# Sliding-window attention and a two-layer MLP on one core: a new order of three entries in the opening's list of transfers, and new planner constants

## The chip, the cores and the metric

The kernel runs on one core of a Trainium2 chip. The metric is device time in microseconds (us) of one launch. A core has five engines that run their own instruction queues in order: TensorE (PE in the profile, its weight loads PEld), VectorE (DVE), ScalarE (ACT), GpSimd (POOL) and SyncE (SP), which here issues nearly all the DMA transfers.

## The reference

Eight batches of eight heads with 576 tokens and 64 numbers per head go through attention with a causal window; the first four heads see the last 32 tokens, the other four see every fourth of the last 128. The result, 4608 tokens of 512 numbers, goes through two matrices with a leaky ReLU between them. All inputs and the output are float32.

```python
rel = pos[:, None] - pos[None, :]
mask_plain = (rel >= 0) & (rel < 32)
mask_dil = (rel >= 0) & (rel < 128) & (rel % 4 == 0)
attn = softmax(where(mask, q @ k.T / 8, -1e9))       # per batch and head
x = (attn @ v).transpose(0, 2, 1, 3).reshape(4608, 512)
h = x @ w_in                                         # 512 x 2048
out = maximum(0.01 * h, h) @ w_out                   # 2048 x 512
```

## The kernel before

Everything is computed in fp16 with float32 accumulation. For each batch the heads are taken in four pairs (`vi` 0 to 3, visited in the order 2, 3, 0, 1). q, k and v are loaded as float32, cast to fp16 (L387 and L386), turned so that the head dimension lies on the partitions (on TensorE for the first two batches, L654 and, for the last 64 tokens, L697; with VectorE's block transpose later, L619 to L631) and copied into a "slot" (L398, L400). Each head pair is then two units of work (`unit`): scores on TensorE (L771 adds the mask in the first two batches, L775), exponential on ACT (L782), the mask multiplied in on VectorE (L786, later batches), for the plain heads a sum of overlapping columns (L802, VectorE or POOL), row sums and values on TensorE (L793, L810), the reciprocal as logarithm and exponential on ACT (L818, L820), and a product on VectorE into `xt` (L831).

The MLP runs over 12 chunks of 384 tokens, three for every two batches. `up` (L850) and `up_pair` (L879) multiply with w_in, and ACT applies the leaky ReLU into `gt` (L865, L891). The last three chunks do it by a scheme of seven block products in place of eight (L1275, evicted at L1287, L1295 and L1302), which needs four sums of w_in blocks (L1201) and sums of tokens (L1226). The first four output tiles of 128 tokens are multiplied with w_out plainly (`down`, L916, four parts per tile, each of which needs two pieces of w_out); the other 32 go in eight groups of four by seven products (L1006), with sums of `gt` blocks on VectorE (L992) and evictions at L1035 and L1043.

Nothing is issued in the order of the code. Every piece of work is a task with an engine (or a choice of engines), a duration, a latency, tasks that it needs, and a priority. `_Plan.forward` simulates the engines: at each step the engine that can start first takes, among its tasks that are ready, the one with the smallest priority. `_Plan.backward` then gives every task the latest time at which it may start, and this becomes its priority for the next pass; nine passes are made and the best is kept. The order of that pass is written out as the program, so each engine's queue is fixed when the program is built. The durations are formulas times the factor of the engine in `MARGIN`; `LAND` scales the latency from a task to its users and `DMA` the time that a transfer takes on the DMA engines. The factors are used only for tasks that start after `CALM` us; before that all are 1. `WHEN` gives each batch a time, from which the first pass's priorities come.

The transfers of the opening are the exception: their priorities are fixed, by their place in the list `FIRST`. In it `q01` stands for q and k of batch 0, head group 1 (two transfers of 512 KB); `v01` for its values; `r0` for the last 64 tokens of q and k of batch 0 (two of 128 KB); `w0` to `w7` for eight pieces of w_in and `w8` to `w15` for eight pieces of w_out (512 KB each); `c` for the mask table. A full stop is the place of the next transfer of an entry of values that has more than one. Fixed priorities do not mean a fixed order: an entry whose buffer is not free is passed by the next one whose buffer is. The pieces of weights are staged in buffers that have another use later (`w_home`, L565): w10, w11 and w12 go into the three thirds of `gt[2]`, which hold w3, w4 and w5 before, and wait for the casts of these. q, k and the last tokens share a ring of five buffers, the values a ring of two. Transfers go out from SyncE through `load` (L373); the planner lets at most eight be under way.

```python
FIRST = ('r0 q01 v01 . q00 w0 v00 . w1 w2 w3 w4 w5 w6 w7 w8 w9 w10 q11 w11 r1 v11 . w12 '
         'w13 q10 v10 w14 . w15 . . c')
...
        t = plan.dma(queue, 0.65, took(n, size) * slow, deps,
```

Of the kernel before, what the change touches and what calls it, by code (L numbers as in the profile page):

```python
# [16 lines left out]
WIN = 32  # L17
ROOM, LATE = 256, 0.5
RAMP = 0.0
WHEN = (0.0, 0.0, 40.0, 70.0, 100.0, 125.0, 150.0, 180.0)  # L20
PASSES = 9
MARGIN = {'ACT': 1.02, 'DVE': 1.062, 'POOL': 1.0, 'PE': 1.0, 'SP': 1.0, 'DMA': 1.133, 'LAND': 1.15}
CALM = 38.8
SEEDS = ()


def _margin(name, at):
    return MARGIN[name] if at > CALM else 1.0
FIRST = ('r0 q01 v01 . q00 w0 v00 . w1 w2 w3 w4 w5 w6 w7 w8 w9 w10 q11 w11 r1 v11 . w12 '
         'w13 q10 v10 w14 . w15 . . c')  # L30


# [38 lines left out]
class _Plan:  # L71
# [22 lines left out]
    def forward(self):  # L94
# [15 lines left out]
        while len(order) < len(self.tasks):  # L110
            best = None
            for eng, cand in waiting.items():
                if not cand:
                    continue
                if eng in cached:
                    got = cached[eng]
                else:
                    here = free.get(eng, 0.0)
                    if eng == "SP":
                        here = max(here, landed[-8] if len(landed) >= 8 else 0.0)  # L120
                        held = ROOM
                        for end, rows in reversed(ends):
                            held -= rows
                            if held < 80:
                                here = max(here, end)
                                break
                    could = []
                    for t in cand:
                        if len(t.choices) > 1:
                            end = max(here, t.ready) + dict(t.choices)[eng] * _margin(eng, here)  # L130
                            if any(max(free.get(e, 0.0), t.ready) + d * _margin(e, here) < end - 0.02
                                   for e, d in t.choices if e != eng):
                                continue
                        could.append(t)
                    if not could:
                        got = None
                    else:
                        at = max(here, min(t.ready for t in could))
                        pick = min(((t.ready + t.soft > at + 1e-9, t.prio, t.n), t)
                                   for t in could if t.ready <= at + 1e-9)  # L140
                        got = (at, pick[1].n, pick[1])
                    cached[eng] = got
# [4 lines left out]
            for e, _ in t.choices:  # L147
                waiting[e].discard(t)
                touched.add(e)
            t.eng, t.start, t.dur = eng, at, dict(t.choices)[eng] * _margin(eng, at)  # L150
            free[eng] = at + t.dur
            if t.service:
# [112 lines left out]
def kernel(  # L265
# [172 lines left out]
    def take_slots(b):  # L438
        for vi in VISITS:
            tn, old = ring("T", NT, users := [])  # L440
            slot_of[b, vi], slot_users[b, vi] = tn, (users, old + t_zero[tn])
# [685 lines left out]
    for b in range(EARLY):  # L1127
        take_slots(b)
    steps = FIRST.split()
    rows, waiting = {}, []  # L1130
# [20 lines left out]
    def attend(b, first, step):  # L1151
        if b >= EARLY:
            take_slots(b)
            for n, g in enumerate((1, 0)):
                load_qk(b, g, first + 2 * step * n - 12)
                load_v(b, g, first + 2 * step * n - 11)
        for n, vi in enumerate(VISITS):
            if b < EARLY and n == b:
                turn_rest(b, first + step * n)
            turn(b, vi, first + step * n)  # L1160
        if b == 0:
            banks = {2: three + [fps[0]], 3: three + [fps[0]], 0: three + hps[1:], 1: three + hps[1:]}
        else:
            banks = dict.fromkeys(VISITS, three + hps if b == 1 else three)
        for n, vi in enumerate(VISITS):
            for u in range(2):
                unit(b, vi, u, first + step * n + 0.5 * step * u, banks[vi])
# [4 lines left out]
    def ups(c, x, n, batches):  # L1172
        if n == 192:
            pool = hps
            for j in range(0, NJ, 2):
                up_pair(c, j, x, n, batches, all_acts[c], pool[j // 2 % len(pool)])
            return
        for j in range(NJ):
            wide_j = c == 0 and j in wide_banks
            ht = wide_banks[j] if wide_j else hps[h_at[0] % 2]  # L1180
            h_at[0] += not wide_j
            up(c, j, x, n, batches, all_acts[c], ht, c == 0)
# [182 lines left out]
    for m in range(B // 2):  # L1365
        for c in range(3 * m, 3 * m + 3):
            gt_free[c] = []
        e, o = 2 * m, 2 * m + 1
        attend(e, WHEN[e], (WHEN[e + 1] - WHEN[e]) / 4 if e else 1.0)
        if 3 * m not in U_SEVEN:  # L1370
# [3 lines left out]
        if m == 0:  # L1374
# [3 lines left out]
            ups(1, 0, 192, [e])  # L1378
            attend(o, WHEN[o], 5.0)
            ups(1, 192, 192, [o])  # L1380
        else:
            attend(o, WHEN[o], 6.5)
            if 3 * m + 1 not in U_SEVEN:
# [74 lines left out]
```

## Time and profile before

| | us |
|---|---|
| median of three runs | 298.97 |
| lowest and highest | 298.30, 300.19 |
| the profiled execution | 299.48 |
| its span, first to last instruction | 297.5 |
| PE busy, of the span | 284.5 |
| DVE busy | 218.1 |
| ACT busy | 218.5 |
| POOL busy | 144.0 |

The span is 1.98 us shorter than the execution's own time. Busy times are sums over the instructions of an engine; matmuls are pipelined and their ends are modelled, so a busy PE is not PE at its peak. Rows of the table by stretches give the length of the stretch and then each engine's busy time in it with the count of instructions. Rows of the timeline give start, duration, engine, line, operation, output and inputs, shape and count, and in brackets the idle time of the engine before the row and what ended it. A row with "SPq" is a transfer's issue, and its duration is the issue's, not the transfer's; the landing is seen in the row of the instruction that waited for it.

### The profile page before, as it was taken

What the parts mean: (1) busy time and instruction counts of PE and PEld (TensorE: products, weight loads), DVE (VectorE), ACT (ScalarE), POOL (GpSimd) and SP (SyncE); (2) the same over time, 40 slices, a digit from 0 to 9 for tenths busy, and PEclk for the clock granted to TensorE, in tenths of its full rate; (3) what the DMA queues carried; (4) which work ended last, traced back from release to release, by engine and by line L of the source; (5) the groups of instructions that cost most, each with busy time, mean ns of one, the idle gap of its engine ahead of it and who ended that gap; (6) DMA issues with size and microseconds to landing.
All of it is one profiled execution on the core that took longest, in us unless ns stands there. A gap on an engine that the chain in (4) does not pass through costs nothing.

```text
span 297.5 us, 7792 instructions
## 1 busy us (share of the span) xinstructions
PE 284.5 (96%) x2975; PEld 225.4 (76%) x2975; DVE 218.1 (73%) x406; ACT 218.5 (73%) x502; POOL 144.0 (48%) x201
## 2 busy tenths in 40 slices
PE   5788989999999999999999999999999999999995
PEld 2665666678667788777777787776789999999984
DVE  6784375975689979738768869999757786587742
ACT  1797469678988884778878876886877787877611
POOL 5545555197778766776885759997100100000000
PEclk9999999999999999999999999999999999999999
DMA  7999999989988989988997998670101210111033
GB/s 216 325 303 402 322 356 249 140 165 169 155 181 175 210 187 149 231 164 173 205 150 197 166 211 160 145 211 3 36 16 53 79 36 2 37 71 39 35 108 106
DMA packets 155973, 47.16 MB, mean 159 GB/s; under 512 B 136736, under 2 KB 153248, under 8 KB 155936
## 3 DMA queue, kind: packets, MB, share of 16 engines
q1 hardware_dynamic: 155248, 46.04, 65.6%
q10 hardware_dynamic: 688, 0.63, 0.7%
q8 instruction: 23, 0.38, 0.6%
q14 instruction: 14, 0.11, 0.1%
HBM read 37.22 MB, written 9.44 MB: 157 GB/s over the span
## 4 chain that ended last, share of the span: by engine, by line
PE 75%; DMA 11%; DVE 5%; SPq 4%; issue 2%; ACT 1%; POOL 1%; DVEq 0%; POOLq 0%
PE hps L850 22%; PE fps L1006 21%; PE tp L1006 8%; PE hps L1275 5%; SPq L373 4%; DMA xt<-in_moe_w_out_dram 3%; PE ops L1275 3%; DMA vst<-in_v_dram 3%; DMA wst<-in_moe_w_in_dram 3%; PE ops L793 3%; PE fps L916 3%; PE hps L879 2%; PE ops L775 2%; DMA stg<-in_k_dram 2%; PE sps L793 1%
## 5 line engine op out<-in xcount | busy, mean ns | idle before, releaser
L850 PE MATMUL hps<-xt,w_in 128*128 128x384 f16 x488 | 95.2, 325 | 1.0 <-DVE w_in L387 0.6
L1006 PEld LDWEIGHTS <-gt 128*128 128x128 f16 x768 | 72.5, 98 | 9.8 <-DVE gt L992 0.4
L865 ACT ACTIVATE gt<-hps 128x384 f16<-128x384 f32 x122 | 59.1, 490 | 20.6 <-PE hps L850 19.5
L850 PEld LDWEIGHTS <-w_in 128*128 128x128 f16 x512 | 45.8, 98 | 23.9 <-issue 1.0
L387 POOL CAST slots<-vst 64x576 f16<-64x576 f32 (+2 forms) x60 | 52.2, 880 | 13.9 <-DVE ee L786 3.9
L387 POOL CAST nat<-stg 128x576 f16<-128x576 f32 (+1 forms) x55 | 41.4, 771 | 20.6 <-PE ops L793 6.8
L1006 PE MATMUL fps<-w_out,gt 128*128 128x256 f16 x368 | 47.0, 272 | 0.0
L786 DVE TENSOR_TENSOR ee<-ee,con 128x384 f16<-128x384 f16 (+1 forms) x48 | 22.2, 464 | 15.5 <-ACT ee L782 15.2
L820 ACT ACTIVATE rc<-rc 128x288 f32<-128x288 f32 x64 | 27.9, 442 | 0.9
L831 DVE TENSOR_TENSOR xt<-ops,rc 128x288 f16<-128x288 f32 x40 | 17.9, 448 | 11.9 <-ACT rc L820 7.7
L775 PEld LDWEIGHTS <-slots 128*128 128x128 f16 x320 | 18.4, 97 | 5.6 <-DVE slots L400 0.9
L400 POOL COPY slots<-turned 64x64 f16<-64x64 f16 (+2 forms) x36 | 19.2, 540 | 6.6 <-DVE turned L619 3.4
L793 PEld LDWEIGHTS <-slots 128*128 128x128 f16 x320 | 17.7, 97 | 4.9 <-issue 1.6
L1035 ACT COPY stg<-fps 128x512 f32<-128x512 f32 (+1 forms) x24 | 12.8, 531 | 11.1 <-PE fps L1006 10.4
L782 ACT ACTIVATE ee<-ops 128x384 f16<-128x384 f32 (+1 forms) x39 | 19.5, 503 | 1.7 <-PE ops L775 0.8
L398 ACT COPY slots<-turned 64x512 f16<-64x512 f16 (+1 forms) x28 | 18.6, 663 | 1.9 <-DVE turned L619 1.5
L818 ACT ACTIVATE rc<-ops 128x288 f32<-128x288 f32 x39 | 15.7, 408 | 5.7 <-PE ops L810 2.8
L802 POOL TENSOR_TENSOR ee<-ee 128x128 f16<-128x128 f16 x9 | 5.4, 601 | 29.2 <-DVE ee L786 29.2
L1302 ACT ACTIVATE gt<-slots 128x384 f16<-128x384 f32 x36 | 18.3, 526 | 0.9 <-DVE slots L1295 0.7
L619 DVE STREAM_TRANSPOSE turned<-nat 128x576 f16<-128x576 f16 x24 | 18.0, 761 | 0.1
L992 DVE TENSOR_TENSOR gt<-gt 128x1024 f16<-128x1024 f16 x21 | 17.1, 819 | 0.4 <-PE fps L1006 0.2
L1275 PEld LDWEIGHTS <-stg 128*128 128x128 f16 x192 | 16.3, 98 | 0.3
(137 smaller groups left out, 554.1 us busy)
## 6 DMA issues: line engine op xcount, KB each, us to landing
out_dram<-osb SPq DMA_DIRECT2D x32, 256.0 KB, 2.7
stg<-in_q_dram SPq DMA_DIRECT2D x48, 144.0 KB, 3.4
stg<-in_k_dram SPq DMA_DIRECT2D x48, 144.0 KB, 3.5
vst<-in_v_dram SPq DMA_DIRECT2D x14, 288.0 KB, 4.2
gt<-in_moe_w_in_dram SPq DMA_DIRECT2D x6, 512.0 KB, 7.1
vst<-in_v_dram SPq DMA_DIRECT2D x24, 128.0 KB, 3.0
stg<-in_q_dram SPq DMA_DIRECT2D x3, 512.0 KB, 9.7
stg<-in_k_dram SPq DMA_DIRECT2D x3, 512.0 KB, 9.5
```

Source lines behind the costliest of these rows:

```text
L387: return ENG[e].tensor_copy(out=dst, in_=src)
L398: nc.scalar.copy(out=dst, in_=src)
L400: ENG[e].tensor_copy(out=dst, in_=src)
L775: nc.tensor.matmul(p_bank[:, c:c + w], slot(tn, KB + 128 * s, 0, 128, [1, 128]), slot(tn, qx, 0, 128, *qd), start=first or not by_pe, stop ...
L782: lambda e: nc.scalar.activation(out=et[:, 0:n], in_=p_bank[:, 0:n], func=AF.Exp, scale=SCALE), prio)
L786: lambda e: nc.vector.tensor_tensor(out=et[:, 0:n], in0=et[:, 0:n], in1=con[:, table:table + n], op=ALU.mult), prio,
L793: nc.tensor.matmul(at(dst, 0, 128, o, *od), lhs(s), et[:, c:c + w], start=i == 0, stop=i == len(steps) - 1, skip_group_check=True)
L820: lambda e: nc.scalar.activation(out=rt, in_=rt, func=AF.Exp, scale=-1.0), prio)
L850: nc.tensor.matmul(ht[:, 0:n], at(w_in, 0, 128, vi * DFF + j // 2 * 256 + j % 2, [2, 128]), at(xt[m % 2], 0, 128, vi * 1152 + x0 + x, [1, n]),
L865: lambda e: nc.scalar.activation(out=gt[c % NG][:, j * n_c + x:j * n_c + x + n], in_=ht[:, 0:n], func=AF.Prelu, alpha=0.01),
L1006: nc.tensor.matmul(bk[:, x:x + HN], tl[:, off + j * step:off + j * step + 128], rhs(j), start=first and x == 0 and j == 0, stop=j == HJ - ...
L1275: nc.tensor.matmul(b[:, i * HT:i * HT + HT], lhs(v, j0 + i), rhs(v), start=first and i == 0 and v == 0, stop=i == 1 and v == 1, skip_group ...
```

## The change

Three places in the opening's list are exchanged: `w11` moves from behind `q11` to ahead of it, and `r1` from ahead of `v11` to behind it. Transfers planned to start before `CALM` get a factor of their own, `LOAD`, 1.003, where it was 1. The factors of VectorE (1.062 to 1.053) and of the latency (1.15 to 1.13), `CALM` (38.8 to 38.1) and the times of the last two batches in `WHEN` (150 to 147.5, 180 to 182.6) are new. No instruction is added or removed by the code; the planner makes another order from the new figures.

```diff
-WHEN = (0.0, 0.0, 40.0, 70.0, 100.0, 125.0, 150.0, 180.0)
+WHEN = (0.0, 0.0, 40.0, 70.0, 100.0, 125.0, 147.5, 182.6)
 PASSES = 9
-MARGIN = {'ACT': 1.02, 'DVE': 1.062, 'POOL': 1.0, 'PE': 1.0, 'SP': 1.0, 'DMA': 1.133, 'LAND': 1.15}
-CALM = 38.8
+MARGIN = {'LOAD': 1.003, 'ACT': 1.02, 'DVE': 1.053, 'POOL': 1.0, 'PE': 1.0, 'SP': 1.0, 'DMA': 1.133, 'LAND': 1.13}
+CALM = 38.1
 SEEDS = ()
 
 
 def _margin(name, at):
-    return MARGIN[name] if at > CALM else 1.0
-FIRST = ('r0 q01 v01 . q00 w0 v00 . w1 w2 w3 w4 w5 w6 w7 w8 w9 w10 q11 w11 r1 v11 . w12 '
+    return MARGIN[name] if at > CALM else MARGIN['LOAD'] if name == 'DMA' else 1.0
+FIRST = ('r0 q01 v01 . q00 w0 v00 . w1 w2 w3 w4 w5 w6 w7 w8 w9 w10 w11 q11 v11 r1 . w12 '
          'w13 q10 v10 w14 . w15 . . c')
```

## The prediction

> **What bounds the kernel now.** I read the page's totals first, then the table by stretches, then the opening engine by engine, because the change edits a list that rules only the first 47 us.
>
> ```profile
> span 297.5 us, 7792 instructions
> PE 284.5 (96%) x2975; PEld 225.4 (76%) x2975; DVE 218.1 (73%) x406; ACT 218.5 (73%) x502; POOL 144.0 (48%) x201
> ```
> ```profile
> 20.00:30.00 10.00, 9.01 (x87) 5.78 (x87) 5.27 (x12) 7.64 (x20) 5.32 (x8) 1.00 1.00 385
> 30.00:40.00 10.00, 8.60 (x78) 5.95 (x76) 4.26 (x12) 4.79 (x10) 4.69 (x6) 1.00 1.10 329
> 40.00:50.00 10.00, 9.98 (x129) 7.77 (x128) 6.63 (x16) 8.87 (x23) 6.18 (x10) 1.00 1.11 310
> 50.00:60.00 10.00, 9.91 (x115) 6.23 (x115) 9.02 (x15) 6.95 (x17) 1.98 (x4) 1.00 0.94 155
> 80.00:100.00 20.00, 19.22 (x198) 13.95 (x197) 18.30 (x31) 17.09 (x41) 14.66 (x21) 1.00 0.92 189
> 180.00:200.00 20.00, 20.00 (x203) 14.94 (x200) 18.87 (x29) 16.86 (x39) 18.54 (x23) 1.00 0.78 172
> 200.00:220.00 20.00, 19.62 (x196) 14.83 (x194) 14.92 (x29) 15.35 (x37) 6.89 (x8) 1.00 0.08 29
> ```
> The columns of a stretch are its length, then busy time of PE, weight loads, DVE, ACT and POOL, the granted clock, the DMA share and GB/s. TensorE is idle 0.99 us in 20 to 30, 1.40 in 30 to 40, 0.02 and 0.09 in the two after that, 0.78 in 80 to 100 and 0.38 in 200 to 220. So from 20 us on there are 3.66 us of visible idle time in these rows, 1.2% of the span. The clock is 1.00 throughout, so nothing is to be had there. Before 50 us the DMA engines are full (share 1.00 to 1.11), so the opening is paced by the order and the rate of the transfers; after 50 us the order of instructions on five engines is fixed by the planner and TensorE is nearly always fed. VectorE is at 18.87 of 20 us just before the last batch ends: the one place where another engine is close to the limit.
>
> That 96% needs a caution. The Trainium skill, "Perfetto Trace Analysis", section "Identifying the Most-Contended Engine", holds matmul busy time for a poor measure and asks for the busy share of weight loads; here that is 76%, and by it 24% of the span would still be open. The rows do not settle how much of that is reachable: the chain of waits shows more lost time than the idle column, as here, where it leaves TensorE for 4.9 us (84.66 to 89.59) although the stretch has 0.78 us of idle.
>
> ```profile
> 84.66 0.49 ACT gt L865
> ...
> 86.14 0.76 issue
> ...
> 89.59 1.05 PE tp L1006 x8
> ```
> I keep 3.66 us as what a better order can win, and let the range go a little past it.
>
> **The change, part by part.** The sum is made against the profiled execution: 299.48 us, of which 297.5 are span and 1.98 lie around it. It is 0.51 above the median of 298.97.
>
> *Everything ahead of place 18 in the list* (r0 to w10) stays. The opening's new factor of 1.003 moves the planned end of 40 us of transfers by about 0.12 us. Cost 0; at worst two neighbouring instructions swap. CALM at 38.1 puts the DMA factor 1.133 on transfers planned in the 0.7 us before 38.8, one or two of them: 0.
>
> *w11 ahead of q11.* The list is not the order: the planner picks the first entry whose buffer is free. w11's staging buffer is the second third of gt[2], which w4 fills, so it waits for w4's two casts.
>
> ```profile
> 24.03 0.61 POOL L387 CAST w_in<-gt 128x512 f16<-128x512 f32 x1 [0.34 <-DMA gt<-in_moe_w_in_dram]
> ```
> ```profile
> 24.19 0.73 DVE L387 CAST w_in<-gt 128x512 f16<-128x512 f32 x1
> 32.93 0.43 DVE L387 CAST nat<-stg 128x512 f16<-128x512 f32 x1 [1.60 <-DMA stg<-in_q_dram]
> 34.22 0.43 DVE L387 CAST nat<-stg 128x512 f16<-128x512 f32 x1 [0.87 <-DMA stg<-in_k_dram]
> 34.96 0.50 DVE L387 CAST rest<-stg 64x256 f16<-64x256 f32 x2 [0.31 <-DMA stg<-in_q_dram]
> 36.70 0.43 DVE L387 CAST w_out<-gt 128x512 f16<-128x512 f32 x1 [1.24 <-DMA gt<-in_moe_w_out_dram]
> 37.04 0.41 DVE L400 COPY slots<-tp 64x512 f16<-64x512 f16 x1
> ```
> ```profile
> 21.34 0.38 SPq L373 DMA_DIRECT2D stg<-in_q_dram  x1
> 22.84 0.38 SPq L373 DMA_DIRECT2D stg<-in_k_dram  x1
> 23.99 2.67 SPq L373 DMA_DIRECT2D stg<-in_q_dram  x1
> 26.77 2.17 SPq L373 DMA_DIRECT2D gt<-in_moe_w_out_dram  x2
> 28.99 1.46 SPq L373 DMA_DIRECT2D stg<-in_k_dram  x1
> 30.54 3.22 SPq L373 DMA_DIRECT2D vst<-in_v_dram  x2
> ```
> These are the casts on POOL and VectorE, and SyncE's issues. w4's last cast ends at 24.92; q11 goes out at 21.34 and its k at 22.84. So w11 cannot pass q11, exactly as w10, which stood ahead of q11 already, was passed by q11, its k and r1's q and left at 26.77. Cost 0. Were it ready after all, q11 would land one 512 KB piece later: 34.22 less 32.93, 1.29 us. Part of the change then does not do what it says.
>
> *r1 behind v11* does act. At 23.99 the queue is free, neither w10 nor w11 is, and the next entry is now v11's main transfer (512 KB) in place of r1's q (128 KB). Its buffer was last used by v01, whose casts are over:
>
> ```profile
> 13.74 0.47 POOL L387 CAST slots<-vst 64x256 f16<-64x256 f32 x1
> ```
> So the order becomes q11, k11, v11, w10, w11, r1 q, r1 k, v11's last tokens. w10 and w11 land later by a large transfer less a small one. By bytes that is 3/4 of 1.29, 0.97 us; by landings r1's q came 0.74 us behind k11 (34.96 less 34.22), so 0.55. I take 0.55, because it is a landing, and keep 0.97 for the range. The Trainium skill, "DMA: Bandwidth & Descriptors", section "Specifications", wants pieces of at least 512 B for full rate; r1's rows are 256 B, and the 0.74 us where bytes alone give 0.32 agree.
>
> What waits for w10 is a stall of TensorE of 1.41 us:
>
> ```profile
> 37.49 0.58 ACT L398 COPY slots<-tp 128x512 f16<-128x512 f16 x1 [1.82 <-DVE slots L400]
> 37.97 0.88 ACT L891 ACTIVATE gt<-hps 128x384 f16<-128x384 f32 x2
> ```
> ```profile
> 34.92 0.39 PE L654 MATMUL tp<-con,nat 128*128 128x128 f16 x4
> ...
> 36.47 1.03 PE L916 MATMUL fps<-w_out,gt 128*128 128x512 f16 x4
> 38.90 0.82 PE L879 MATMUL hps<-xt,w_in 128*128 128x192 f16 x8 [1.41 <-ACT gt L891]
> 39.65 0.40 PE L697 MATMUL tp<-con,rest 64*128 64x64 f16 x8
> ...
> 41.52 0.33 PE L771 MATMUL ops<-con 128*128 128x192 f16 x3
> ```
> VectorE stands 1.24 us before w10's cast; the copy of a transposed tile is queued behind it; ACT's copy waits 1.82 us for that, its evictions are queued behind, and TensorE stands 1.41 us for a bank. Two ends: with the queue order kept, the stall grows by 0.55 (0.97); with w10 due later in the plan, the copy is placed ahead of the cast and the 1.41 go, unless v11's casts, now due at about 36, take the same seat. I take -0.6, near the middle of -1.4 and +0.55 and a little to the gain's side, since the transpose that the copy reads ends at 35.31 in any case.
>
> ```profile
> 39.26 0.47 DVE L387 CAST rest<-stg 64x256 f16<-64x256 f32 x2
> 40.03 1.19 DVE L387 CAST slots<-vst 64x256 f16<-64x256 f32 x3 [0.30 <-DMA vst<-in_v_dram]
> ```
> r1's k lands after w11 and r1's q: it takes v11's old place, 0.8 us later than now at most (v11's first casts start at 40.03 on VectorE, those of r1 at 39.26). Its transposes (39.65) and the second batch's first scores (41.52) go later by that; three more pairs of up matmuls and a down part lie beside them in 40 to 50, where TensorE has 9.98 of 10. Cost 0, bound +0.8. v11's casts leave 40 to 43 for the slack time of 36 to 38: worth at most the 0.11 us idle in 40 to 60.
>
> *The constants* (VectorE 1.062 to 1.053, landing 1.15 to 1.13, WHEN of the last two batches) change no instruction and no duration; they redraw the order after 38 us. WHEN only seeds the first of nine passes. What they can win is 0.78 + 0.38 us. What they can lose is worked out from VectorE:
>
> ```profile
> L992 DVE TENSOR_TENSOR gt<-gt 128x1024 f16<-128x1024 f16 x21 | 17.1, 819 | 0.4 <-PE fps L1006 0.2
> L802 DVE TENSOR_TENSOR ee<-ee 128x128 f16<-128x128 f16 x15 | 6.6, 439 | 0.3
> L1201 DVE TENSOR_TENSOR stg<-w_in 128x2048 f16<-128x2048 f16 x2 | 2.5, 1246 | 0.0
> ```
> The plan gives L992 0.63 x 1.062 = 0.669 us and L802 0.319; the trace has 0.819 and 0.439. VectorE already runs behind its plan, and 1.053 asks 0.9% more of it, 0.16 us over the 18.87. I take 0 for the redraw: present lost time is small, and a plan of the same kind will lose about as much.
>
> Sum: 0 + 0 - 0.6 + 0 + 0 = -0.6, so 298.9 for an execution like the profiled one, 298.4 against the median.
>
> **The rivals.** *Slower: VectorE becomes the bound before the last batch ends.* In 180 to 200 it has 1.13 us free, and the four sums of w_in (1.25 us each), the 0.82 us sums of the down groups and the last batch's multiplies share it. If two sums of w_in and two of L992 are drawn ahead of the last batch's work, its tokens come 2 x 1.25 + 2 x 0.82 = 4.1 us late. It decides once this exceeds what TensorE still has queued for earlier chunks; 0.38 us of idle there says the reserve is nearly used. With the opening's +0.55: 299.0 + 4.1 + 0.55, about 303.6. For it: the rows above and a plan that becomes more hopeful. Against: TensorE has 20.00 of 20 in the stretch with the fullest VectorE. Chance 0.30.
>
> *Faster: the redraw removes the idle.* All 3.66 us from 20 us on go: 299.0 - 3.7 = 295.3. For it: every one of these gaps is a queue order, not a lack of data, the 1.41 us above all. Against: it takes luck in five places. Chance 0.27.
>
> *The reorder is void*, if readiness already rules there: the redraw alone, within 1% of 299. It is inside my own forecast's 0.43.
>
> **How the numbers follow.** 1% is 3 us, about what a measurement of this kernel can tell from no change. Likeliest is 298.4 at 0.43, whose own range is 296.2 to 301.5 (-1.4 and -1.2 below, +0.97, +0.8 and one more stall of 0.8 above). Over all cases 294.8 to 303.8: the faster rival's 295.3 with a little past it, and the slower's 303.6. Left out are several such losses at once and gains beyond the visible idle, about 2 in 10. Faster 0.27, same 0.43, slower 0.30.
>
> **What would show it.** SyncE issues v11's main transfer right behind k11 near 24 us, and r1's q and k behind two w_out pieces; w11 is still behind q11. w10's casts start near 37.2. Idle in 30 to 40 is below 1.4 if the copy went ahead, above 1.9 if not. The second batch's first scores start at 41.5 to 42.5. Idle from 60 to 280 stays near 1.2. I am wrong if w11 leaves before q11, if a stall over 2 us stands in 30 to 60, or if TensorE idles over 3 us between 180 and 225 behind VectorE.

## The result and the profile after

| | before | changed |
|---|---|---|
| median, us | 299.43 (20 runs) | 300.84 (20 runs) |
| lowest and highest, us | 297.08, 301.39 | 298.23, 302.79 |
| ratio to before | | 1.0048, 95% interval 1.0025 to 1.0070 |
| profiled execution, us | 299.48 | 300.19 |

The changed kernel is slower by half a per cent, 1.4 us between the medians. The forecast was 0.6 us faster; the measured time lies in the stated range and within the 1% that was given 0.43, but on the other side of the kernel before.

The page of the changed kernel, its totals:

```profile
span 298.4 us, 7773 instructions
PE 284.5 (95%) x2974; PEld 225.3 (75%) x2974; DVE 219.3 (73%) x413; ACT 216.7 (73%) x499; POOL 141.7 (47%) x197
```
TensorE's busy time is the same 284.5 us. The span grew by 0.9 us, so all of it is idle time. The table by stretches of the changed kernel (columns as in the prediction) says where:

```profile
0.00:10.00 10.00, 6.47 (x50) 3.29 (x51) 6.67 (x18) 3.64 (x7) 5.43 (x14) 1.00 0.83 252
10.00:20.00 10.00, 7.99 (x133) 6.24 (x131) 8.77 (x20) 9.63 (x23) 5.98 (x10) 1.00 1.09 336
20.00:30.00 10.00, 9.35 (x75) 5.61 (x73) 4.50 (x12) 7.59 (x20) 5.55 (x8) 1.00 1.03 383
30.00:40.00 10.00, 8.72 (x77) 6.01 (x76) 5.22 (x15) 5.55 (x12) 6.04 (x10) 1.00 1.09 339
40.00:50.00 10.00, 10.00 (x143) 7.97 (x141) 6.37 (x15) 7.94 (x20) 3.38 (x5) 1.00 1.12 285
50.00:60.00 10.00, 9.44 (x94) 5.45 (x93) 9.12 (x15) 6.08 (x16) 4.70 (x5) 1.00 0.95 152
80.00:100.00 20.00, 18.10 (x179) 12.78 (x177) 17.11 (x28) 16.93 (x40) 15.27 (x23) 1.00 0.97 205
200.00:220.00 20.00, 19.17 (x192) 14.18 (x189) 17.77 (x30) 14.37 (x36) 10.85 (x10) 1.00 0.12 42
```
The first two rows of the same table for the kernel before:

```profile
0.00:10.00 10.00, 5.99 (x31) 2.54 (x32) 6.40 (x15) 2.55 (x5) 5.56 (x15) 1.00 0.81 247
10.00:20.00 10.00, 7.85 (x128) 6.22 (x126) 8.32 (x20) 9.45 (x22) 5.30 (x10) 1.00 1.01 305
```
Idle time of TensorE, before and after: 6.16 and 5.54 us in 0 to 20; 2.39 and 1.93 in 20 to 40; 0.11 and 0.56 in 40 to 60; 0.78 and 1.90 in 80 to 100; 0.38 and 0.83 in 200 to 220. Up to 60 us the changed kernel is 0.63 us ahead, but 0.62 of that lies in the first 20 us, ahead of the entries that changed places; from 20 to 60 us the two are level (2.50 and 2.49 us idle). In the two late stretches it loses 1.12 + 0.45 = 1.57 us. The difference, 0.94, is the growth of the span.

SyncE's queue of the changed kernel in the opening:

```profile
20.68 0.57 SPq L373 DMA_DIRECT2D stg<-in_q_dram  x1
21.36 0.64 SPq L373 DMA_DIRECT2D stg<-in_k_dram  x1
22.40 2.72 SPq L373 DMA_DIRECT2D vst<-in_v_dram  x1
25.23 2.28 SPq L373 DMA_DIRECT2D gt<-in_moe_w_out_dram  x2
27.56 1.68 SPq L373 DMA_DIRECT2D stg<-in_q_dram  x1
29.29 1.34 SPq L373 DMA_DIRECT2D stg<-in_k_dram  x1
```
q11, its k, v11, then w10 and w11, then r1: the order that the prediction gave. w11 did not pass q11.

The late loss, in the changed kernel's rows of VectorE, GpSimd and TensorE. The brackets give the idle time of an engine before the row and what ended it:

```profile
92.18 1.93 DVE L786 TENSOR_TENSOR ee<-ee,con 128x384 f16<-128x384 f16 x1
```
```profile
91.00 1.64 POOL L400 COPY slots<-turned 64x64 f16<-64x64 f16 x3
92.59 0.69 POOL L625 COPY slots<-turned 128x576 f16<-128x576 f16 x1
93.24 0.66 POOL L387 CAST nat<-stg 128x576 f16<-128x576 f32 x1
```
```profile
88.55 1.05 PE L1006 MATMUL tp<-w_out,gt 128*128 128x256 f16 x8 [0.79 <-DVE gt L992]
94.16 0.33 PE L793 MATMUL sps<-ee,con 128*128 128x96 f16 x5 [0.73 <-DVE ee L786]
```
The mask multiply at 92.18 ran beside an unbroken run of GpSimd copies and a cast, 91.00 to 93.90 us, and took 1.93 us; the row sums at 94.16 waited for it. At 88.55 the down group had waited for VectorE's sums.

### The profile page after: what moved, and what is told of

Same layout as the page of the kernel before. It is cut to its first block, busy times and chain, and to the rows that moved or that the text cites. A ratio compares the mean times of both kernels' runs of the same rounds, so it can differ in the third digit from the quotient of the medians.

```text
span 298.4 us, 7773 instructions
## 1 busy us (share of the span) xinstructions
PE 284.5 (95%) x2974; PEld 225.3 (75%) x2974; DVE 219.3 (73%) x413; ACT 216.7 (73%) x499; POOL 141.7 (47%) x197
## 4 chain that ended last, share of the span: by engine, by line
PE 74%; DMA 10%; SPq 5%; DVE 5%; ACT 2%; issue 1%; POOL 1%; POOLq 0%; DVEq 0%
PE fps L1006 22%; PE hps L850 21%; PE tp L1006 8%; SPq L373 5%; PE hps L1275 5%; DMA stg<-in_k_dram 5%; PE ops L1275 3%; PE ops L793 3%; DMA vst<-in_v_dram 3%; PE fps L916 3%; DMA wst<-in_moe_w_in_dram 3%; PE hps L879 2%; PE ops L775 2%; PE sps L793 2%; DVE ee L786 1%; PE sps L1275 1%
## 5 line engine op out<-in xcount | busy, mean ns | idle before, releaser
L387 POOL CAST nat<-stg 128x576 f16<-128x576 f32 (+1 forms) x55 | 42.8, 792 | 31.1 <-DVE ee L786 11.9
L387 POOL CAST slots<-vst 64x576 f16<-64x576 f32 (+2 forms) x59 | 50.4, 863 | 12.4 <-DMA vst<-in_v_dram 3.3
L786 DVE TENSOR_TENSOR ee<-ee,con 128x384 f16<-128x384 f16 (+1 forms) x48 | 23.9, 500 | 13.7 <-ACT ee L782 13.3
L1035 ACT COPY stg<-fps 128x512 f32<-128x512 f32 (+1 forms) x25 | 13.4, 536 | 13.2 <-PE fps L1006 12.4
L398 ACT COPY slots<-turned 64x512 f16<-64x512 f16 (+1 forms) x29 | 19.3, 665 | 0.6 <-DVE turned L619 0.2
L1006 PE MATMUL fps<-wst,gt 128*128 128x256 f16 x128 | 16.4, 272 | 0.0
```

The lines of the kernel that those rows point to most:

```text
L387: return ENG[e].tensor_copy(out=dst, in_=src)
L398: nc.scalar.copy(out=dst, in_=src)
L786: lambda e: nc.vector.tensor_tensor(out=et[:, 0:n], in0=et[:, 0:n], in1=con[:, table:table + n], op=ALU.mult), prio,
L1006: nc.tensor.matmul(bk[:, x:x + HN], tl[:, off + j * step:off + j * step + 128], rhs(j), start=first and x == 0 and j == 0, stop=j == HJ - ...
```

## The experiments

Theory A says that the opening is no worse and that the order drawn for the rest is; theory B that the moved entries of the list cost the time. All ratios are to the kernel before, measured beside it on the same chip in 6 or 12 runs, with a 95% interval. None of these kernels is shown to be 2% slower; an interval that leaves out 1 is called slower or faster here.

| kernel | ratio | interval |
|---|---|---|
| opening of after, rest of before | 0.9980 | 0.9945 to 1.0015 |
| opening of before, rest of after | 1.0036 | 1.0004 to 1.0068 |
| after to 140 us, then before | 1.0099 | 1.0067 to 1.0131 |
| before to 140 us, then after | 1.0023 | 0.9991 to 1.0054 |
| list alone | 1.0161 | 1.0126 to 1.0195 |
| constants alone | 1.0168 | 1.0120 to 1.0216 |
| whole change without LOAD | 1.0172 | 1.0121 to 1.0223 |
| transfers moved, all else as before | 1.0163 | 1.0121 to 1.0205 |
| changed, one wait added | 1.0037 | 1.0007 to 1.0067 |
| changed, GpSimd never stands back | 1.0169 | 1.0116 to 1.0222 |
| changed, GpSimd stands back more | 1.0145 | 1.0108 to 1.0182 |
| before, GpSimd stands back more | 1.0016 | 0.9991 to 1.0041 |

**Four spliced orders.** The two plans were written down as a table (task, engine, start, duration, added waits), and a kernel was built from one plan's tasks that start before a cut and, behind them, the rest in the other plan's order.

```diff
-    order = plan.run()
+    order = plan.given(TABLE)
```


> The changed kernel's order on every engine for the work planned before 58 us, then the order of the kernel before for all that is left. Theory A (the loss lies in the order drawn after the opening; the opening itself gained): about 0.6 us under the kernel before, ratio 0.998, and the idle time of TensorE in 80 to 100 us is near before's 0.78. Theory B (the loss lies in the opening, the moved list entries): as slow as the changed kernel, ratio 1.005.

> The reverse: the order of the kernel before for the work planned before 58 us, then the changed kernel's order. Theory A: slower than the changed kernel by the opening's gain, about 301.4, ratio 1.007, idle of TensorE in 80 to 100 us near 1.9. Theory B: like the kernel before, ratio 1.000.

Two stretches of each; first the opening of after with the rest of before, then the reverse:

```profile
30.00:40.00 10.00, 9.71 (x87) 6.80 (x86) 5.52 (x14) 6.71 (x15) 5.90 (x10) 1.00 1.08 342
80.00:100.00 20.00, 19.27 (x203) 14.45 (x201) 18.42 (x33) 17.33 (x40) 15.74 (x21) 1.00 0.96 201
200.00:220.00 20.00, 19.61 (x211) 15.32 (x210) 14.58 (x31) 15.10 (x37) 5.49 (x6) 1.00 0.05 15
```
```profile
30.00:40.00 10.00, 9.82 (x87) 6.83 (x85) 5.45 (x14) 5.57 (x13) 5.02 (x8) 1.00 1.09 349
80.00:100.00 20.00, 18.08 (x180) 12.84 (x176) 17.60 (x28) 16.86 (x41) 15.68 (x23) 1.00 0.92 197
200.00:220.00 20.00, 19.13 (x189) 14.14 (x187) 17.89 (x29) 14.32 (x36) 10.04 (x10) 1.00 0.12 42
```
The late idle time goes with the late order: 0.73 and 0.39 us with before's, 1.92 and 0.87 with after's, whatever the opening was. The times agree: the first is level with the kernel before or slightly ahead, the second is slower. Theory B is out: the loss of the changed kernel does not go with its opening. The opening's gain of 0.6 us that theory A named is what the first ratio comes to (0.2% of 299), but it is not shown: that interval takes in 1, and the second kernel came out at 1.0036 and not 1.007.

The row of 30 to 40 us says more. The second kernel has before's opening, the same order on every engine, and 0.18 us of idle there where the kernel before had 1.40.

> The changed kernel's order for work planned before 140 us, that of the kernel before from there on; 25 of 1954 tasks lie on the other side of the cut in the other plan. If the loss is that of 80 to 100 us alone, as slow as the changed kernel, ratio 1.005. If half of it is that of 200 to 220 us (TensorE idle 0.83 against 0.38), ratio 1.002.

> The reverse: the order of the kernel before up to 140 us, then the changed kernel's. If the loss is that of 80 to 100 us alone: ratio 1.000. If half of it is that of 200 to 220 us: ratio 1.003, TensorE idle in 200 to 220 near 0.83.

The second has 0.72 us of idle in 80 to 100 and 0.85 in 200 to 220, as its two halves promise, and a ratio of 1.0023 with an interval that takes in 1 and the 1.003 expected. The first, at 1.0099, is slower than both readings. Its profile shows why:

```profile
80.00:100.00 20.00, 18.09 (x180) 12.84 (x178) 17.30 (x28) 16.87 (x40) 15.39 (x22) 1.00 0.93 198
140.00:160.00 20.00, 18.69 (x182) 13.53 (x181) 14.33 (x27) 16.08 (x38) 16.23 (x23) 1.00 0.90 173
```
1.91 us as in the changed kernel, and 1.31 at the cut, where the two plans do not fit together. It says nothing of the share of 200 to 220.

**The parts alone.** Three kernels, each a piece of the change:

```diff
 list alone, the kernel before with
+FIRST = ('r0 q01 v01 . q00 w0 v00 . w1 w2 w3 w4 w5 w6 w7 w8 w9 w10 w11 q11 v11 r1 . w12 '
 constants alone, the changed kernel with
+FIRST = ('r0 q01 v01 . q00 w0 v00 . w1 w2 w3 w4 w5 w6 w7 w8 w9 w10 q11 w11 r1 v11 . w12 '
 without LOAD, the changed kernel with
-MARGIN = {'LOAD': 1.003,
+MARGIN = {'LOAD': 1.0,
```


> The kernel before with the new list alone, all constants as before. The transfers go in the changed order (v11 ahead of w10 and w11). Theory A: the opening is no slower than before's (TensorE idle in 20 to 60 us at most 2.5 us, before 2.5), and the rest is a new draw whose stalls decide: a ratio anywhere from 0.997 to 1.010. Theory B: slower by 0.5% with the loss before 60 us.

> The changed kernel's constants with the list of the kernel before. Theory C (a schedule of this kind is a draw, and the kernel before is one picked for its short time; any single edit redraws the order after the opening and most draws are slower): slower than before, ratio 1.005 to 1.015, with stalls of TensorE of over 0.5 us each at new places between 50 and 220 us. Theory D (the constants as such are better or worse by themselves, the list is the cost): the list alone cost 1.6%, the whole change 0.5%, so the constants alone would be faster than before, ratio about 0.990.

> The changed kernel with the opening's factor 1.003 back at 1. It moves the planned end of the opening's transfers by about 0.1 us. Theory C: this alone redraws the order, and the time leaves the changed kernel's by 0.5% or more, most likely upward: ratio to before 1.008 or above. Theory D: 0.1 us of planned time is worth nothing: ratio 1.005 as for the changed kernel.

All three are slower than before by 1.6 to 1.7%, 4.8 to 5.1 us, and slower than the whole change. The constants do not pay for the list: alone they cost as much. And 0.3% on the opening's transfers, 0.1 us of planned time, is worth 1.2% between the last kernel and the whole change. What the three have in common is only that the planner drew a new order. Theory C's direction holds in both kernels that it was put to, with 1.0168 a little above the 1.005 to 1.015 that it gave for the constants; theory D's 0.990 and 1.005 did not come. List alone lies outside both of its expectations, with a ratio above 1.010 and 3.77 us of idle in 20 to 60 us where at most 2.5 was allowed. Two of its new stalls:

```profile
50.00:60.00 10.00, 7.93 (x98) 5.03 (x95) 8.49 (x13) 6.49 (x17) 2.88 (x5) 1.00 1.02 161
80.00:100.00 20.00, 17.09 (x178) 12.51 (x176) 17.67 (x32) 14.86 (x37) 14.49 (x21) 1.00 0.91 190
```
2.07 and 2.91 us of idle where the kernel before has 0.09 and 0.78. The kernel without LOAD has 1.99 in 80 to 100 and 1.99 in 200 to 220; the second is one stall, and the clock fell behind it (last section). Constants alone has 2.42 us in 80 to 100.

**The transfers alone, nothing redrawn.** The five transfers change places in SyncE's queue; every other queue stays as before.

```diff
     order = plan.run()
+    first = {round(t.prio, 1): t for t in order if t.service and t.prio < -1400}
+    moved = [first[p] for p in (-1478.0, -1482.0, -1480.0, -1479.0, -1478.9)]
+    for t, x in zip(moved, sorted(t.start for t in moved)):
+        t.start = x
+    order.sort(key=lambda t: (t.start, t.n))
```


> The kernel before with five of SyncE's transfers in the changed order (v11, w10, w11, r1's q, r1's k in place of r1's q, w10, w11, r1's k, v11) and every other queue untouched, so that nothing is redrawn. Theory G (the step of the prediction: w10 lands about 0.55 us later and, with the queues as they were, what is queued behind its cast waits as much longer): ratio 1.001 to 1.003, TensorE idle in 30 to 40 us 0.5 us above that of the same order without the move (0.18 to 1.40 us in four profiles). Theory H (other work covers it, and what the move does is below the scatter of the opening): ratio 0.999 to 1.001, idle in 30 to 40 us within 0.18 to 1.40.

Neither came: the ratio is 1.0163. Its rows on VectorE, ACT and TensorE, and the stretch behind them:

```profile
39.22 0.49 DVE L387 CAST rest<-stg 64x256 f16<-64x256 f32 x2 [5.79 <-DMA stg<-in_q_dram]
39.63 0.69 DVE L387 CAST w_out<-gt 128x512 f16<-128x512 f32 x1
40.25 0.40 DVE L400 COPY slots<-tp 64x512 f16<-64x512 f16 x1
```
```profile
40.68 0.59 ACT L398 COPY slots<-tp 128x512 f16<-128x512 f16 x1 [5.56 <-DVE slots L400]
```
```profile
42.09 1.44 PE L879 MATMUL hps<-xt,w_in 128*128 128x192 f16 x8 [5.14 <-ACT gt L891]
```
```profile
40.00:50.00 10.00, 7.91 (x81) 6.23 (x80) 6.85 (x17) 5.69 (x14) 5.23 (x10) 0.68 1.11 300
```
VectorE's queue has the cast of r1's q ahead of w10's cast and of the copies that ACT and TensorE wait for. r1's q now lands behind w10 and w11, so VectorE stands 5.79 us and TensorE 5.14, and the clock is at half for some time behind that (0.68 in this stretch). From 58 us on the kernel runs as before: its idle time in 80 to 100 and 200 to 220 is 0.72 and 0.39 us. The list's new order is affordable only because the planner then draws the queues anew. In the changed kernel VectorE casts q, k and v11, then copies, then casts w10:

```profile
33.59 1.29 DVE L387 CAST slots<-vst 64x256 f16<-64x256 f32 x3 [0.93 <-DMA vst<-in_v_dram]
34.89 0.86 DVE L400 COPY slots<-tp 128x512 f16<-128x512 f16 x2
35.78 0.43 DVE L387 CAST w_out<-gt 128x512 f16<-128x512 f32 x1
```
**The collisions of VectorE with GpSimd.** The plan's `share` makes a GpSimd cast wait for a mask multiply that it would run beside. It covers neither GpSimd's copies nor VectorE's other work. One such wait was added by hand; in another kernel all were taken out; in two more the rule was widened, on the changed kernel and on the kernel before. The order stays as it was in each. (For the wider rule the helper of the copies also hands back its instruction, so that a wait can be tied to it.)

```diff
 one wait:
     order = plan.run()
+    by = {t.n: t for t in order}
+    by[764].yields.append(by[779])
 never:
-        self.share(order)
 more:
-            if t.eng == "DVE" and t.kind in ("m",):
+            if t.eng == "DVE" and t.kind in ("m", "A", "T"):
-            elif t.eng == "POOL" and t.kind == "cast" and last is not None:
+            elif t.eng == "POOL" and t.kind in ("cast", "") and last is not None:
```


> The changed kernel with one wait added: GpSimd's copy of the turned q of batch 3's first pair (L625, at 92.6 us) waits for VectorE's mask multiply of the same stretch, which took 1.93 us beside it where others take 0.4. Theory A1 (the collision of VectorE with GpSimd is what TensorE waits for at 94 us): the multiply takes under 0.9 us, the 0.73 us of idle before the row sums go, and the time falls by about 1 us against the changed kernel, ratio to before 1.001. Theory A2 (the order alone, the unit simply stands late): the multiply may shrink, the time stays at ratio 1.005.

The multiply and the two stretches with it:

```profile
92.38 0.67 DVE L786 TENSOR_TENSOR ee<-ee,con 128x384 f16<-128x384 f16 x1
```
```profile
80.00:100.00 20.00, 18.82 (x187) 13.54 (x186) 16.92 (x28) 17.63 (x42) 15.81 (x22) 1.00 0.94 201
100.00:120.00 20.00, 19.66 (x214) 16.60 (x212) 17.14 (x33) 13.05 (x29) 11.43 (x15) 1.00 0.81 154
```
The collision is what TensorE waited for at 94 us: without it the multiply takes 0.67 us and the idle time of the stretch falls by 0.72. Half of that, 0.34, is lost again right behind. The ratio, 1.0037, lies between the two expectations and its interval holds both of them, 1.001 and 1.005; a gain in time is not shown.

> The changed kernel, its order untouched, without the 27 waits by which GpSimd's casts stand back for VectorE's mask multiplies. Theory E (VectorE instructions that read two tensors slow down beside GpSimd, and that is part of what TensorE waits for): the multiplies' mean rises from 500 ns to 600 or more, TensorE's idle time in 80 to 100 and 200 to 220 us grows, ratio to before 1.010 or above. Theory F (these waits matter little; the late stalls are the order's): mean may rise, ratio stays 1.003 to 1.007.

> The changed kernel, its order untouched, with 64 such waits in place of 27: GpSimd's casts and copies stand back for the multiplies and also for the sums of the down groups and of w_in (L992, L1201). Theory E: the multiplies and sums shrink (L992 from 0.82 towards 0.70 us), idle in 80 to 100 falls to about 1.1 and in 200 to 220 to about 0.4, ratio 1.001. Theory F, or a wait that costs as much as it saves because GpSimd falls behind: ratio 1.005 or above with idle at new places.

> The same wider rule on the kernel before (66 waits in place of 21), its order untouched. Theory E: idle in 80 to 100 and 200 to 220 falls from 1.16 towards 0.5, ratio 0.998. Theory F: 1.000 or slower, since this order was short with the stalls as they are.

Without the waits the same multiply takes 2.53 us and the time rises to 1.0169:

```profile
93.14 2.53 DVE L785 TENSOR_TENSOR ee<-ee,con 128x384 f16<-128x384 f16 x1
94.18 1.28 POOL L386 CAST nat<-stg 128x576 f16<-128x576 f32 x2
```
(The lines of this kernel are one less.) TensorE's idle time in 80 to 120 us is 4.14 us, in the changed kernel 1.90. Since the order is the same, the same matmuls can be compared: four of `up` start at 79.59 us in the changed kernel and at 80.64 here, eight at 120.84 and at 124.84. So 2.95 of the 3.8 us by which this profile's span is longer are lost between the two. The collisions matter: theory E holds in that direction, though two of its signs failed. The multiplies' mean rose only to 526 ns, not to 600, and the idle time in 200 to 220 us fell, to 0.42.

In the other direction it fails. With 64 waits the multiplies shrink to a mean of 479 ns, but the sums of the down groups do not (759 ns for the 21 that the prediction shows at 819, where the changed kernel has 720), idle is 0.64 us in 100 to 120 and 1.71 in 200 to 220, most of it one wait for a sum on GpSimd, and the ratio is 1.0145:

```profile
205.70 0.22 PE L809 MATMUL ops<-ee,con 128*128 128x128 f16 x1 [1.40 <-POOL ee L801]
```
Not all of the loss is the price of the waits: the four matmuls of 79.59 us start at 81.18 in this profile, so 1.59 of its 2.8 us are there before any of the stretches in question. On the kernel before, the wider rule leaves the idle time of the two stretches at 1.01 us (1.16 without it, 0.5 expected by theory E) and changes nothing in the time that can be told from 1.

## Why the prediction was wrong

*The redraw at 0* is the step that failed: "present lost time is small, and a plan of the same kind will lose about as much". The order drawn for the work behind the opening costs 0.36% (0.04 to 0.68), some 1.1 us, with the same opening ahead of it. It shows as 1.57 us more idle time in 80 to 100 and 200 to 220 us, at the same size in each profile that has this order there unaltered; the sign named for it, idle from 60 to 280 us near 1.2, came out at 2.73. And 0 was no fair value for a redraw: of four orders drawn from parts of this change or from all of it, three lose 1.6 to 1.7% and the best 0.5%. The kernel before was a short one among these neighbours, so a new order of the same kind should have been priced above it. That the change stayed within 1% all the same was luck of the draw.

The plan itself hinted at it. In the tables of the spliced kernels the last transfer is issued at 294.04 us by the plan of before and at 294.75 by the changed one (the tables add 1000 to every start behind the cut), 0.7 us later with smaller factors for VectorE and for the latency. And I called VectorE's 18.87 of 20 us in 180 to 200 the one place near the limit; 18.30 in 80 to 100, where most of the loss came, stood in the same table.

*The stall behind w10 at -0.6* rested on one execution. I read 1.41 us of idle from one execution and took it for a property of the order. Four profiles with the same opening order have 1.40, 0.18, 0.82 and 0.32 us of idle in 30 to 40 us, 0.68 in the mean; six with the changed opening have 0.29 to 1.28, 0.73 in the mean. The stall ahead of L879 itself is 1.41, 0.18, absent and 0.32. The queue is the same in the four; what differs is when transfers land: VectorE waits 1.24, 0.51, 0.60 and 0.51 us for w10. The opening as a whole is worth -0.55% to +0.15% by the first splice, which takes in -0.6 us; that it gains is not shown.

*What I left out of that step*: the cast of r1's q, which stood in my own quoted rows at 34.96, ahead of w10's cast in VectorE's queue. r1's move was priced for the scores at +0.8 at most; with the queues kept the five moved transfers cost 4.8 us, the half clock included, and r1's q is what VectorE waits for. The planner avoided it, so it cost the forecast nothing, but the 0.97 at the upper side for "the queue order kept" was wrong by a factor of five. The 0.55 for the landing was sound: from VectorE's cast of q11 to GpSimd's of w10 it takes 4.11 us there, and 3.50 to 3.80 in the four profiles with before's opening. The casts of w10 in the changed kernel came at 35.24 and 35.78 us, not near 37.2, since q11 had landed 2.03 us earlier in that execution. (My own forecast's range adds up to 296.4 at its lower end, not 296.2; nothing hangs on it.)

*Right*: w11 void, v11 ahead of both pieces and r1 last, no cost for the second batch's scores (41.15 after, 41.52 before, by the rows of L771). The copy did go ahead of w10's cast (34.89 and 35.78). The slower rival's mechanism is there in its place, VectorE late before the last batch ends, with two sums of w_in drawn among the last batch's work, at a tenth of its price: 0.45 us more idle time than before where I had 4.1:

```profile
199.99 1.68 DVE L1201 TENSOR_TENSOR stg<-w_in 128x2048 f16<-128x2048 f16 x1
201.96 1.79 DVE L1201 TENSOR_TENSOR stg<-w_in,stg 128x2048 f16<-128x2048 f16 x1
209.82 0.36 PE L793 MATMUL sps<-ee,slots 128*128 128x64 f16 x5 [0.83 <-DVE ee L786]
```
Its argument, that VectorE runs behind its plan and the new factor asks more, was not tested by itself.

*Open*: what makes one drawn order lose at 80 to 100 us and another not. One collision accounts for 0.72 us of idle there; removing it did not shorten the time measurably.

## What to carry to other kernels

Where a planner writes out the order, an edit of any of its constants is a new draw: price it by the spread of a few neighbours, not by the lost time of the one that is in hand, which may well be there because it was short. Before a stall of one execution enters a sum, look for it in a second one of the same program. And when a transfer is moved back, look through every in-order queue for its consumer and for what stands behind that.

## What the runs showed of the hardware

A VectorE instruction with two tensor inputs, 0.37 us in the median (48 multiplies of the changed kernel), took 1.93 us beside a run of GpSimd copies and casts and 2.53 us with GpSimd's waits taken out. Both times it ended 0.21 us after a run of GpSimd's instructions without a pause (94.11 after 93.90, 95.67 after 95.46). The Trainium skill, "GPSIMD Engine Reference", section "1. Specifications", says that GpSimd's interfaces to the on-chip memory SBUF are shared with VectorE and that VectorE instructions with two inputs from there contend; both inputs of the multiply lie there, the traces agree, and add the size.

The granted clock fell to half behind some stalls, and how long the stall was does not settle it. Behind the 5.14 us of idle in the kernel with the moved transfers it was 0.50 until about 46 us. In the kernel without LOAD it fell behind 1.99 us:

```profile
208.30 0.26 PE L810 MATMUL ops<-ee,con 128*128 128x128 f16 x1 [1.99 <-POOL ee L802]
208.72 1.90 PE L1006 MATMUL tp<-t,gt 128*128 128x256 f16 x8
```
```profile
208.00:210.00 2.00, 1.70 (x13) 1.32 (x13) 1.99 (x4) 0.85 (x2) 2.00 (x3) 0.58 0.04 8
```
The eight matmuls at 208.72 took 1.90 us, where the same eight take 1.04 with the full clock. List alone stood 2.10 us ahead of its row sums and kept the clock:

```profile
89.28 0.35 PE L793 MATMUL sps<-ee,slots 128*128 128x96 f16 x5 [2.10 <-DVE ee L786]
```
```profile
88.00:90.00 2.00, 0.72 (x10) 0.55 (x10) 2.00 (x5) 0.04 (x1) 1.22 (x3) 1.00 1.09 174
```
The opening has the same difference from one execution to the next. Two profiles with before's opening, first the kernel before with the wider rule for GpSimd, then the splice with the rest of after:

```profile
10.00:12.00 2.00, 2.00 (x25) 1.98 (x25) 0.87 (x3) 1.52 (x5) 0.00 (x0) 0.52 1.03 376
12.00:14.00 2.00, 1.82 (x27) 1.45 (x25) 1.74 (x6) 1.95 (x6) 1.21 (x3) 0.63 1.18 266
```
```profile
10.00:12.00 2.00, 1.79 (x33) 1.38 (x30) 1.17 (x4) 1.98 (x6) 0.19 (x2) 1.00 1.10 408
```
Half the clock for 3.41 us in one, none of it in the other. Four of the fourteen profiles have it there, two of them kernels whose ratios take in 1 and two that lose 1.6 to 1.7%, so it is not what tells these apart. Nor does it explain the spread of the kernel before. One such stretch takes the mean clock of an execution to 0.994. Of the executions of this kernel beside the others, the 24 with a mean of 0.995 or less took 299.5 us on average and the 54 with 0.998 or more 299.1, but these alone run from 296.7 to 301.2.

The clock records of the traces settle more than the stalls do. Each stretch of half clock inside a kernel lasts 3.41 us, or twice that in the kernel with the moved transfers (39.63 to 46.46). In the kernel without LOAD it starts at 10.37 and at 208.34 us, 58 times 3.413 us apart. So the clock looks to be set at fixed intervals of 3.41 us. In the interval that ends at 208.34 TensorE was idle for the whole 1.99 us, 58%. In list alone, whose intervals are fixed by its own fall at 9.61 us, a boundary at 88.12 cuts the 2.10 us in two, and neither side has more than 45%. Worked out for all fourteen profiles past the opening, each interval of 58% idle or more is followed by half the clock, and none of 52% or less is. The opening is stricter: half the clock followed where the first interval at the full clock was 32 to 51% idle (four profiles), and not where it was 28% or less (ten). Why the opening differs is open.

The Trainium skill, "TensorE: Matmul & The Clock Gate", Part 1, puts the drop to half rate after one idle window of about 3.4 us. The length of the interval agrees; an interval that was 58% idle was enough here, and the measurement decides.
